# Gated MLP in a decode step's forward and backward pass: order of w2's rows, sums by row groups, and two vectors spread by matmuls of repeated columns

## The chip, the cores and the metric

The kernel runs on one core of one Trainium2 chip. The metric is the device time of one execution in microseconds (us); smaller is better. A core has TensorE (PE in the profile, its weight loads PEld), VectorE (DVE), ScalarE (ACT), GpSimd (POOL) and SyncE (SP, which here only issues transfers), and 16 DMA engines that move data between the chip's memory and the on-chip buffers. Matmul results land in PSUM, everything else lies in SBUF.

## The reference: what is computed

One token `x` (640 numbers) is normalised and goes through attention over a cache and through a gated MLP; both results are added to `x`. Then the gradients of this sum are taken with respect to nearly all inputs. Cut to what matters:

```python
xn  = layernorm(x)                                   # 1 x 640
q   = (xn @ wq) per head                             # 32 heads of 128
p   = softmax(q @ k_cache^T * 128**-0.5)             # 32 x 8192
o   = p @ v_cache
A   = o @ wo
gate, up = xn @ w1, xn @ w3                          # 1728 each
h   = silu(gate) * up
B   = h @ w2
out = x + A + B
# outputs: out, and the gradients of out (weighted by grad_out) for
# x, k_cache, v_cache, wq, wo, w1, w3, w2
```

`k_cache` and `v_cache` hold 32 x 8192 x 128 bf16 numbers each (67 MB), and so do their gradients. For the MLP, with `g = grad_out`: `dh = w2 @ g`, `dup = dh * silu(gate)`, `dgate = dh * up * silu'(gate)`, `dw2 = h x g`, `dw1 = xn x dgate`, `dw3 = xn x dup` (outer products), and `dxn = w1 @ dgate + w3 @ dup`.

## The kernel before

The instructions of each engine run in the order in which the program writes them (a manual schedule), so the text of the kernel is the order of every queue. There are three stages.

**Loads and set-up (L107 to L286).** SP issues loads in this order: x, w2 in two parts (L192, L193), w1 (L194), the last 64 rows of w2 (w2r, L195), w3 (L196), wq and wo of the first heads, K and V of heads 0 and 1, wq and wo of the next heads. F = 1728 = 13 x 128 + 64: the MLP's long axis is cut into NF = 13 blocks of 128 and a REST of 64, so NB = 14 columns hold a vector of 1728. Entry q of block b is element 13 q + b (`block`, L562). The rest is the last 64 elements. xn is kept as 5 columns of 128 (`xn_col`), NC = 5.

**MLP (L558 to L712).** The weights lie as [128, 5, 1728] (w1t, w3t) and [128, 13, 640] (w2t, with w2r beside it). In the order of the text:

- `dh_product` (L567): w2 times g on DVE, summed over columns by matmuls with the identity, three calls; the last one uses w2r. `dh_reduce` (L579) folds the sums into `dhc` (dh, 14 columns).
- `gate_sums` (L582): 70 matmuls with one moving column each, block by block, the five row groups `ci` inside; its weights are read from w1t with a step of 13 elements. Then tanh on ACT and small operations on DVE give silu and `dup`.
- `spread(1, dup, ...)` (L595): turns 14 columns into a row of 1728 that all partitions hold (`bc_sb`). DVE multiplies the identity by the repeated columns (L598, L600), which gives a wide diagonal `diag`; four matmuls with a weight of ones (L604) put its column sums on all partitions, in PSUM; ACT and DVE copy them to `bc_sb` (L605).
- `gate_sums` again, for `up` with w3; `dx_part(1, w3t, ...)` (L607): w3 times `bc_sb` on DVE (L609), summed by matmuls into `dx_ps` (L612); `keep_sums`, `dgate`; `spread(0, dgate, ())`, all copies on ACT; the rest of `dx_part(1, ...)`; `grad(1, w3t)` (L616, L618), which overwrites w3t with its gradient; the store of dw3 from POOL (L658) and the load of K for head 2 into the same buffers behind it (L659).
- `ps_out` (L664) for h @ w2, the w2 gradients on ACT (L622), `prep_steps(0)` (L289), which makes q and the gradient of o for heads 0 to 3, `dx_part(0, w1t, ...)`, `grad(0, w1t)`, and the store of dw1 (L693).

**Heads (L707 to L840).** For each of 32 heads, DVE multiplies K by q and V by the gradient of o in halves (`product`, L414), PE sums these by matmuls with the identity (L416), and softmax and its gradient follow. `outer` (L436 on DVE, L430 on ACT) writes the 2 MB gradients of V and K of this head to `ot` tiles; POOL stores them (L443). SP loads K three heads and V two heads ahead, as buffers come free. Four `ot` buffers exist, three for K and two for V. Some of them first hold what the MLP needs: w1t, w2t and w3t take K's buffers, and `dbc` (with diag, bc_sb and w2r) takes one of the `ot` buffers. The pool `ps_w` has three PSUM banks, which the MLP's sums take in turn; `ps_acc` has two, which the heads' products use.

At the end the last gradients and the two outputs of 640 are stored (L802 to L841).

Of the kernel before, what the change touches and what calls it, by code (L numbers as in the profile page):

```python
# [9 lines left out]
BF16 = mybir.dt.bfloat16  # L10
F32 = mybir.dt.float32
ALU = mybir.AluOpType
# [4 lines left out]
P = 128  # L17
# [4 lines left out]
def kernel(  # L22
# [22 lines left out]
    nc = tc.nc  # L45
# [3 lines left out]
    D = A_x.shape[2]  # L49
    F = B_w1.shape[1]  # L50
    assert DH == P and D % P == 0 and SK % (2 * P) == 0
    NC = D // P
# [8 lines left out]
    NF, REST = divmod(F, P)  # L61
    NB = NF + 1
# [4 lines left out]
    WIDE = 4  # L67
# [11 lines left out]
    opool = ctx.enter_context(tc.tile_pool(name="op", bufs=4))  # L79
    small = ctx.enter_context(tc.tile_pool(name="small", bufs=2))  # L80
    ps_pers = ctx.enter_context(tc.tile_pool(name="ps_pers", bufs=1, space=PSUM))
    ps_acc = ctx.enter_context(tc.tile_pool(name="ps_acc", bufs=2, space=PSUM))
    ps_s = ctx.enter_context(tc.tile_pool(name="ps_s", bufs=1, space=PSUM))
    ps_o = ctx.enter_context(tc.tile_pool(name="ps_o", bufs=1, space=PSUM))
    ps_w = ctx.enter_context(tc.tile_pool(name="ps_w", bufs=3, space=PSUM))
# [17 lines left out]
    with tc.manual_schedule(engines=ORDERED):  # L103
# [80 lines left out]
        w3t = kpool.tile([P, NC, F], BF16, name="w3t", tag="K")  # L184
        w1t = kpool.tile([P, NC, F], BF16, name="w1t", tag="K")
        w2t = kpool.tile([P, NF, D], BF16, name="w2t", tag="K")
        dbc = opool.tile([P, 4 * F + D], BF16, name="dbc", tag="o")
        diag = dbc[:, 0:2 * F].rearrange("p (w f) -> p w f", w=2)
        bc_sb = dbc[:, 2 * F:4 * F].rearrange("p (w f) -> p w f", w=2)
        w2r = dbc[:, 4 * F:]  # L190
        nc.gpsimd.memset(w2r, 0.0)
        nc.sync.dma_start(w2t[:, 0:W2A, :], w2_v[:, 0:W2A, :])  # L192
        nc.sync.dma_start(w2t[:, W2A:NF, :], w2_v[:, W2A:NF, :])  # L193
        nc.sync.dma_start(w1t[:], w1_v)  # L194
        nc.sync.dma_start(w2r[0:REST, :], B_w2[NF * P:F, :])  # L195
        nc.sync.dma_start(w3t[:], w3_v)  # L196
        load_wq(0)
        load_wo(0, nc.sync)
# [8 lines left out]
        ident_bf = consts.tile([P, P], BF16, name="ident_bf")  # L207
# [6 lines left out]
        ones_bf = consts.tile([P, P], BF16, name="ones_bf")  # L214
# [38 lines left out]
        xn_col_bf = consts.tile([P, NC], BF16, name="xn_col_bf")  # L253
# [4 lines left out]
        for i, row in enumerate((x_row, g_row)):  # L258
            for ci in range(NC):
                nc.tensor.matmul(ps_xg[:, 2 * i, ci:ci + 1], lhsT=row[:].rearrange("o (p c) -> o c p", c=NC)[:, ci, :],  # L260
                                 rhs=ones_bf[0:1, 0:1], start=True, stop=True)
                nc.tensor.matmul(ps_xg[:, 2 * i + 1, ci:ci + 1], lhsT=row[:, ci * P:(ci + 1) * P],
                                 rhs=ones_bf[0:1, 0:1], start=True, stop=True)
# [127 lines left out]
        def new_head(h):  # L391
            st = Head()
            st.h = h
            st.g, st.hh = divmod(h, GH)
            st.G = grp[st.g]
            st.K, st.V = kv_tiles.pop(h)
            hs[h] = st
            return st
# [163 lines left out]
        def block(ap, b):  # L562
            if b < NF:
                return ap[:, 0:NF * P].rearrange("p (q b) -> p b q", b=NF)[:, b, :]
            return ap[:, NF * P:F]
# [13 lines left out]
        def dh_reduce(b0, nb, dh_ps):  # L579
            nc.vector.tensor_reduce(dhc[:, b0:b0 + nb], dh_ps[:], AX.X, ALU.add)  # L580

        def gate_sums(name, wt):  # L582
            ps = ps_w.tile([P, NB], F32, name=name, tag="w")
            for b in range(NB):
                rows = P if b < NF else REST
                for ci in range(NC):
                    nc.tensor.matmul(ps[0:rows, b:b + 1], lhsT=block(wt[:, ci, :], b),
                                     rhs=xn_col_bf[:, ci:ci + 1], start=(ci == 0), stop=(ci == NC - 1))
            return ps

        def keep_sums(dst, ps):
            nc.vector.tensor_copy(dst[:, 0:NF], ps[:, 0:NF])
            nc.vector.tensor_copy(dst[0:REST, NF:NB], ps[0:REST, NF:NB])

        def spread(wi, vec, on_v):  # L595
            nc.vector.tensor_copy(dgu2[:, wi], vec)
            by_run = diag[:, wi, 0:NF * P].rearrange("p (q b) -> p q b", b=NF)
            nc.vector.tensor_tensor(by_run, ident_bf[:].unsqueeze(2).to_broadcast([P, P, NF]),  # L598
                                    dgu2[:, wi, 0:NF].unsqueeze(1).to_broadcast([P, P, NF]), ALU.mult)
            nc.vector.tensor_scalar(diag[:, wi, NF * P:F], ident_bf[:, 0:REST], vec[:, NF:NB], None, ALU.mult)  # L600
            for k in range(4):
                c = slice(k * F // 4, (k + 1) * F // 4)
                bc_ps = ps_w.tile([P, F // 4], F32, name="bc_ps", tag="w")
                nc.tensor.matmul(bc_ps[:], lhsT=ones_bf[:], rhs=diag[:, wi, c], start=True, stop=True)  # L604
                (nc.vector.tensor_copy if k in on_v else nc.scalar.copy)(bc_sb[:, wi, c], bc_ps[:])  # L605

        def dx_part(wi, wt, c0, n):  # L607
            T = tpool.tile([P, n, F], BF16, name="T13", tag="T")
# [16 lines left out]
        gate, up, th, sig, silu, hcol, t1, dgate, dup = (sm_f[:, i, :] for i in range(9))  # L625
        dhc = small.tile([P, NB], F32, name="dhc", tag="Pf")
        dgu2 = small.tile([P, 2, NB], BF16, name="dgu2", tag="Pf")
# [5 lines left out]
        dh2 = dh_product(2 * W2A, NB - 2 * W2A)  # L633
        dh_reduce(*dh1)
        dh_reduce(*dh2)
        keep_sums(gate, gate_sums("gate_ps", w1t))
        nc.scalar.activation(th, gate, ACTF.Tanh, scale=0.5)
        nc.vector.tensor_scalar(sig, th, 0.5, 0.5, ALU.mult, ALU.add)
        nc.vector.tensor_tensor(silu, gate, sig, ALU.mult)
        nc.vector.tensor_tensor(dup, dhc[:], silu, ALU.mult)  # L640
        spread(1, dup, (1, 3))
        nc.vector.tensor_scalar(t1, sig, -1.0, 1.0, ALU.mult, ALU.add)
        nc.vector.tensor_tensor(t1, t1, gate, ALU.mult)
        nc.vector.tensor_scalar(t1, t1, 1.0, None, ALU.add)
        nc.vector.tensor_tensor(t1, t1, sig, ALU.mult)
        nc.vector.tensor_tensor(t1, dhc[:], t1, ALU.mult)
        up_ps = gate_sums("up_ps", w3t)
        dx_ps = ps_w.tile([P, NC, DR1], F32, name="dx_ps", tag="w")
        dx_part(1, w3t, 0, 2)
        keep_sums(up, up_ps)  # L650
        nc.vector.tensor_tensor(dgate, t1, up, ALU.mult)
        nc.vector.tensor_tensor(hcol, silu, up, ALU.mult)
        nc.vector.tensor_copy(hcol_bf[:], hcol)
        spread(0, dgate, ())
        dx_part(1, w3t, 2, 2)
        dx_part(1, w3t, 4, 1)
# [4 lines left out]
        for b in range(NB):  # L661
            rows, src = (P, w2t[:, b, :]) if b < NF else (REST, w2r)
            for ci in range(NC):
                nc.tensor.matmul(ps_out[:, ci:ci + 1], lhsT=src[0:rows, ci * P:(ci + 1) * P],  # L664
                                 rhs=hcol_bf[0:rows, b:b + 1], start=(b == 0 and ci == 0), stop=(b == NB - 1),
                                 skip_group_check=True)
# [58 lines left out]
        for h in range(H - 1):  # L725
            n = new_head(h + 1) if h + 1 < H else None
            c = hs.pop(h)
# [51 lines left out]
        c = hs.pop(H - 1)  # L779
# [34 lines left out]
        for ci in range(NC):  # L814
            k, c = divmod(ci * P, WIDE_COLS)
# [56 lines left out]
```

## Time and profile before

| what | value |
|---|---|
| time, median of 3 runs | 720.65 us (719.62 to 720.72) |
| the profiled execution's own time | 720.15 us |
| its span, first to last instruction | 718.4 us |
| busy in the span: PE, DVE, ACT, POOL | 555.2, 631.4, 479.3, 49.5 us |
| moved by DMA | 303.32 MB, mean 422 GB/s |
| share of 16 DMA engines: SP's queue, POOL's queue, ACT's queue | 51.0%, 45.1%, 3.5% |
| mean granted clock of TensorE | 0.886 |
| dw3's store issued; dw1's store issued | 38.96 us; 46.54 us |
| first product of head 0 starts on DVE | 46.16 us |
| DVE's last instruction starts; last store issued | 707.99 us; 708.29 us |

How to read it: the busy share of an engine is an average over stages. The page's second part cuts the span into 40 slices of 18 us and gives for each the busy tenths of the engines and DMA and the rate. The fourth part follows the chain that ended last back from the end. The windows give the same numbers for stretches of one's own choice. A wait is given as who waited, for whom, how long in total, how often, and the longest.

### The profile page before, as it was taken

How to read it: one execution, taken by the hardware profiler on the slowest of the kernel's cores; microseconds unless marked ns; L12 is line 12 of the kernel's file. 1: busy time of each engine (PE TensorE's matmuls, PEld its weight loads, DVE VectorE, ACT ScalarE, POOL GpSimd, SP SyncE). 2: the span in 40 equal slices, each digit the busy share in tenths (PEclk: the TensorE clock that was granted, in tenths of full speed). 3: DMA queues.
4: the chain of work that ended last, by engine and by line, in shares of the span. 5: the costliest groups of instructions: out<-in, count | busy, mean ns of one | idle time of the engine just before them, and what ended most of it. 6: DMA issues, size and time to landing. Idle time of an engine off the chain costs nothing.

```text
span 718.4 us, 9840 instructions
## 1 busy us (share of the span) xinstructions
PE 555.2 (77%) x3516; PEld 274.3 (38%) x3516; DVE 631.4 (88%) x723; ACT 479.3 (67%) x1456; POOL 49.5 (7%) x91
## 2 busy tenths in 40 slices
PE   5787788888788786775888788497877888888862
PEld 3653343333344333332443344143433334333331
DVE  5789999999999996896799999499999989899992
ACT  2165677696779756695487866469677857678551
POOL 0010000000001210000000110000000000000100
PEclk9699989999998988997799979779899889999995
DMA  8999999999999999999999999999999999999997
GB/s 351 415 426 424 431 430 401 430 429 428 434 428 430 430 425 424 425 427 428 430 426 432 430 427 422 428 428 429 429 429 431 430 428 433 427 430 431 428 422 304
DMA packets 27694, 303.32 MB, mean 422 GB/s; under 512 B 3264, under 2 KB 3974, under 8 KB 9982
## 3 DMA queue, kind: packets, MB, share of 16 engines
q1 hardware_dynamic: 13490, 154.89, 51.0%
q0 software_dynamic: 10960, 137.72, 45.1%
q10 hardware_dynamic: 3196, 10.10, 3.5%
q8 instruction: 27, 0.44, 0.2%
q14 instruction: 21, 0.17, 0.1%
HBM read 151.34 MB, written 151.34 MB: 421 GB/s over the span
## 4 chain that ended last, share of the span: by engine, by line
DVE 41%; DMA 36%; PE 15%; ACT 5%; issue 1%; SPq 0%; POOL 0%; DVEq 0%; ACTq 0%; POOLq 0%
DMA Kt<-in_A_k_cache_dram 20%; DVE T L414 19%; DVE ot L436 12%; DMA out_dram<-ot 10%; DMA lane_pad<-in_A_wq_dram 4%; PE ob L485 4%; PE psDP L416 4%; ACT ot L430 3%; PE psS L416 3%; DMA dbc<-in_B_w_dram 2%; DVE S_sb L457 1%; DVE DP_sb L511 1%; PE ps_od L501 1%; PE dx_ps L612 1%; DVE P L476 1%
## 5 line engine op out<-in xcount | busy, mean ns | idle before, releaser
L416 PE MATMUL psDP<-T,ident_bf 128*128 128x512 bf16 x512 | 158.1, 465 | 67.4 <-DVE T L414 67.2
L416 PEld LDWEIGHTS <-ident_bf 128*128 128x128 bf16 x1024 | 107.9, 109 | 205.3 <-issue 131.1
L430 ACT ACTIVATE ot<-qs_g,Uf 128x128 bf16<-128x128 bf16 x496 | 151.7, 394 | 43.5 <-DVE Uf L523 26.5
L414 DVE TENSOR_TENSOR T<-Kt,qs_g 128x4096 bf16<-128x4096 bf16 x64 | 146.4, 2287 | 14.9 <-DMA Kt<-in_A_k_cache_dram 13.7
L430 ACT ACTIVATE ot<-do_g,Pf 128x128 bf16<-128x128 bf16 x504 | 154.0, 389 | 7.0 <-DMA out_dram<-ot 6.0
L414 DVE TENSOR_TENSOR T<-Vt,do_g 128x4096 bf16<-128x4096 bf16 x64 | 146.0, 2282 | 5.6 <-DMA Vt<-in_A_v_cache_dram 5.6
L416 PE MATMUL psS<-T,ident_bf 128*128 128x512 bf16 x512 | 126.4, 391 | 10.0 <-DVE T L414 10.0
L436 DVE TENSOR_TENSOR ot<-qs_g,U 128x3072 bf16<-128x3072 bf16 (+1 forms) x64 | 113.2, 1768 | 12.4 <-DMA out_dram<-ot 12.3
L436 DVE TENSOR_TENSOR ot<-do_g,P 128x3072 bf16<-128x3072 bf16 (+1 forms) x64 | 112.9, 1764 | 7.1 <-DMA out_dram<-ot 6.1
L443 POOL DMA_DIRECT2D out_dram<-ot x60 | 32.2, 536 | 548.4 <-DVE Uf L523 315.1
L485 PE MATMUL ob<-Vt,P 128*4 128x512 bf16 x512 | 62.2, 386 | 0.0
L485 PE MATMUL ob<-Kt,U 128*4 128x512 bf16 x512 | 60.5, 379 | 1.3 <-DVE U L518 1.3
L478 ACT ACTIVATE Pf<-E,rZ 128x16 f32<-128x16 f32 x32 | 9.7, 304 | 57.9 <-DVE rZ L474 57.9
L542 ACT ACTIVATE dq_diag<-ident_bf,odq 128x128 bf16<-128x128 bf16 x32 | 12.8, 401 | 50.9 <-DVE odq L538 50.9
L501 PEld LDWEIGHTS ps_od<-pick,wide 128*128 128x128 f32 x256 | 42.2, 233 | 8.3 <-issue 2.8
L501 PE MATMUL ps_od<-pick,wide 128*128 128x2 f32 x256 | 37.2, 267 | 0.5 <-ACT wide L493 0.5
L461 PE MATMUL sm<-ident_f,mrow 128*128 128x128 f32 x64 | 15.9, 331 | 24.1 <-DVE mrow L459 24.1
L485 PEld LDWEIGHTS <-U 128*4 128x4 bf16 x512 | 19.8, 84 | 37.4 <-DVE U L518 6.9
L485 PEld LDWEIGHTS <-P 128*4 128x4 bf16 x512 | 20.6, 85 | 24.7 <-issue 1.5
L493 ACT COPY wide<-ob 128x256 f32<-128x256 f32 x64 | 20.0, 362 | 10.5 <-PE ob L485 10.5
L306 ACT COPY woT<-ps_t 128x512 bf16<-128x512 bf16 x40 | 23.0, 576 | 5.2 <-PE ps_t L301 4.5
L457 DVE TENSOR_REDUCE S_sb<-psS 128x64 f32<-128x512 f32 x32 | 21.9, 685 | 4.5 <-PE psS L416 4.5
(173 smaller groups left out, 549.9 us busy)
## 6 DMA issues: line engine op xcount, KB each, us to landing
out_dram<-ot POOLq DMA_DIRECT2D x60, 2048.0 KB, 24.1
Kt<-in_A_k_cache_dram SPq DMA_DIRECT2D x32, 2048.0 KB, 26.5
Vt<-in_A_v_cache_dram SPq DMA_DIRECT2D x32, 2048.0 KB, 20.5
out_dram<-ot SPq DMA_DIRECT2D x8, 1024.0 KB, 13.3
out_dram<-wo_g ACTq DMA_DIRECT2D x6, 640.0 KB, 15.2
wo_g<-in_A_wo_dram ACTq DMA_DIRECT2D x6, 640.0 KB, 15.6
wq<-in_A_wq_dram SPq DMA_DIRECT2D x2, 1280.0 KB, 33.7
w1t<-in_B_w_dram SPq DMA_DIRECT2D x1, 2160.0 KB, 12.7
```

The costliest lines, as they stand in the source:

```text
L306: nc.scalar.copy(woT[:], ps_t[:])
L414: nc.vector.tensor_tensor(T[:], src[:, :, ds_], vec[:, ds_].unsqueeze(1).to_broadcast([P, J, DHH]), ALU.mult)
L416: nc.tensor.matmul(ps[:], lhsT=ident_bf[:], rhs=T[:, :, RUN * i:RUN * (i + 1)], start=(half == 0 and i == 0), stop=(half == 1 and i == DHH ...
L430: nc.scalar.activation(st.ot[half][:, JH - ACT_J + j].rearrange("p a b -> p (a b)"), vec, ACTF.Copy, scale=wf[:, half, j:j + 1])
L436: nc.vector.tensor_tensor(st.ot[half][:, 0:n], vec.rearrange("p (a b) -> p a b", b=2).unsqueeze(1).to_broadcast([P, n, DH // 2, 2]), w2[:, ...
L443: nc.gpsimd.dma_start(dst.rearrange("p j d -> p (j d)"), st.rows[:])
L457: nc.vector.tensor_reduce(st.S[:], st.ps["S"][:], AX.X, ALU.add)
L461: nc.tensor.matmul(st.sm[:, 8:8 + P], lhsT=mrow[:].to_broadcast([P, P]), rhs=ident_f[:], start=True, stop=True, skip_group_check=True)
L485: nc.tensor.matmul(ob[c0:c0 + WIDE, :], lhsT=w2[:, WIDE * q:WIDE * (q + 1), 0], rhs=src[:, WIDE * q:WIDE * (q + 1), :].rearrange("p j d -> ...
L493: nc.scalar.copy(part[:], ob[:, i * (WIDE // 2) * DH:(i + 1) * (WIDE // 2) * DH])
L501: nc.tensor.matmul(st.od, lhsT=st.wide[i][:, b * DH:(b + 1) * DH], rhs=pick[:, r, :], start=(r == 0), stop=(r == WIDE - 1), skip_group_che ...
L542: nc.scalar.activation(dq_diag[:], ident_bf[:], ACTF.Copy, scale=odq[:, 1:2])
```

## The change

Four edits, all in the loads and the MLP:

1. The load of w2's last rows (w2r) is issued before w1's, no longer after it.
2. `gate_sums` now runs the row groups `ci` outside and the 14 blocks inside, into a PSUM tile that the caller gives. For `up`, the first row group (14 matmuls) is issued right after the gate's sums, ahead of `spread(1, ...)`, and the other four (56) after it. `up_ps` now lies in the pool `ps_acc`.
3. `spread` builds no diagonal. For each of 13 blocks (and the rest) one matmul takes the column of that block, repeated 128 times, as weights, and the identity as the moving operand; four blocks share a PSUM bank. The sums are then copied to `bc_sb` with a step of 13 elements in the destination. The fourth chunk has one block and the rest, and two copies.
4. `dbc` loses the room for the diagonal.

```diff
-        dbc = opool.tile([P, 4 * F + D], BF16, name="dbc", tag="o")
-        diag = dbc[:, 0:2 * F].rearrange("p (w f) -> p w f", w=2)
-        bc_sb = dbc[:, 2 * F:4 * F].rearrange("p (w f) -> p w f", w=2)
-        w2r = dbc[:, 4 * F:]
+        dbc = opool.tile([P, 2 * F + D], BF16, name="dbc", tag="o")
+        bc_sb = dbc[:, 0:2 * F].rearrange("p (w f) -> p w f", w=2)
+        w2r = dbc[:, 2 * F:]
...
         nc.sync.dma_start(w2t[:, W2A:NF, :], w2_v[:, W2A:NF, :])
+        nc.sync.dma_start(w2r[0:REST, :], B_w2[NF * P:F, :])
         nc.sync.dma_start(w1t[:], w1_v)
-        nc.sync.dma_start(w2r[0:REST, :], B_w2[NF * P:F, :])
         nc.sync.dma_start(w3t[:], w3_v)
...
-        def gate_sums(name, wt):
-            ps = ps_w.tile([P, NB], F32, name=name, tag="w")
-            for b in range(NB):
-                rows = P if b < NF else REST
-                for ci in range(NC):
-                    nc.tensor.matmul(ps[0:rows, b:b + 1], lhsT=block(wt[:, ci, :], b),
-                                     rhs=xn_col_bf[:, ci:ci + 1], start=(ci == 0), stop=(ci == NC - 1))
-            return ps
+        def gate_sums(ps, wt, rows_of):
+            for ci in rows_of:
+                for b in range(NB):
+                    rows = P if b < NF else REST
+                    nc.tensor.matmul(ps[0:rows, b:b + 1], lhsT=block(wt[:, ci, :], b), rhs=xn_col_bf[:, ci:ci + 1],
+                                     start=(ci == 0 and b == 0), stop=(ci == NC - 1), skip_group_check=True)
...
         def spread(wi, vec, on_v):
             nc.vector.tensor_copy(dgu2[:, wi], vec)
-            by_run = diag[:, wi, 0:NF * P].rearrange("p (q b) -> p q b", b=NF)
-            nc.vector.tensor_tensor(by_run, ident_bf[:].unsqueeze(2).to_broadcast([P, P, NF]),
-                                    dgu2[:, wi, 0:NF].unsqueeze(1).to_broadcast([P, P, NF]), ALU.mult)
-            nc.vector.tensor_scalar(diag[:, wi, NF * P:F], ident_bf[:, 0:REST], vec[:, NF:NB], None, ALU.mult)
-            for k in range(4):
-                c = slice(k * F // 4, (k + 1) * F // 4)
-                bc_ps = ps_w.tile([P, F // 4], F32, name="bc_ps", tag="w")
-                nc.tensor.matmul(bc_ps[:], lhsT=ones_bf[:], rhs=diag[:, wi, c], start=True, stop=True)
-                (nc.vector.tensor_copy if k in on_v else nc.scalar.copy)(bc_sb[:, wi, c], bc_ps[:])
+            by_block = bc_sb[:, wi, 0:NF * P].rearrange("p (q b) -> p b q", b=NF)
+            for k, b0 in enumerate(range(0, NF, WIDE)):
+                n = min(WIDE, NF - b0)
+                bc_ps = ps_w.tile([P, WIDE, P], F32, name="bc_ps", tag="w")
+                for b in range(b0, b0 + n):
+                    nc.tensor.matmul(bc_ps[:, b - b0, :], lhsT=dgu2[:, wi, b:b + 1].to_broadcast([P, P]), rhs=ident_bf[:],
+                                     start=True, stop=True, skip_group_check=True)
+                if b0 + n == NF:
+                    nc.tensor.matmul(bc_ps[:, n, 0:REST], lhsT=dgu2[:, wi, NF:NB].to_broadcast([P, P]),
+                                     rhs=ident_bf[:, 0:REST], start=True, stop=True, skip_group_check=True)
+                copy = nc.vector.tensor_copy if k in on_v else nc.scalar.copy
+                copy(by_block[:, b0:b0 + n, :], bc_ps[:, 0:n, :])
+                if b0 + n == NF:
+                    copy(bc_sb[:, wi, NF * P:F], bc_ps[:, n, 0:REST])
...
-        keep_sums(gate, gate_sums("gate_ps", w1t))
+        gate_ps = ps_w.tile([P, NB], F32, name="gate_ps", tag="w")
+        gate_sums(gate_ps, w1t, range(NC))
+        keep_sums(gate, gate_ps)
+        up_ps = ps_acc.tile([P, NB], F32, name="up_ps", tag="acc")
+        gate_sums(up_ps, w3t, range(1))
         nc.scalar.activation(th, gate, ACTF.Tanh, scale=0.5)
...
-        up_ps = gate_sums("up_ps", w3t)
+        gate_sums(up_ps, w3t, range(1, NC))
         dx_ps = ps_w.tile([P, NC, DR1], F32, name="dx_ps", tag="w")
```

## The prediction

> **What bounds the kernel now.** I read the page first, then the windows, then DVE's waits. The page's slices, bytes and chain:
>
> ```profile
> DVE  5789999999999996896799999499999989899992
> DMA  8999999999999999999999999999999999999997
> GB/s 351 415 426 424 431 430 401 430 429 428 434 428 430 430 425 424 425 427 428 430 426 432 430 427 422 428 428 429 429 429 431 430 428 433 427 430 431 428 422 304
> HBM read 151.34 MB, written 151.34 MB: 421 GB/s over the span
> DVE 41%; DMA 36%; PE 15%; ACT 5%; issue 1%; SPq 0%; POOL 0%; DVEq 0%; ACTq 0%; POOLq 0%
> ```
>
> The DMA row is 9 in every slice but the first and the last, and the rate stands near 428 GB/s from the second slice to the last but one. The DVE row has holes, at 6, 4 and 8. The last line is only one chain, and its DVE share says that DVE often ended last, not that DMA was free then. The windows (columns: PE, PEld, DVE, ACT, POOL busy us, granted clock, DMA share, GB/s) show both at once:
>
> ```profile
> 60.00:245.00 185.00, 152.55 (x932) 72.05 (x932) 180.35 (x195) 138.48 (x436) 13.64 (x24) 0.93 1.01 427
> 400.00:500.00 100.00, 76.38 (x449) 36.71 (x448) 85.53 (x94) 69.54 (x215) 9.55 (x15) 0.86 1.01 427
> 110.00:115.00 5.00, 4.86 (x35) 2.63 (x34) 5.00 (x5) 5.00 (x17) 0.00 (x0) 1.00 0.98 374
> 705.00:710.00 5.00, 1.65 (x7) 1.25 (x7) 1.57 (x11) 0.00 (x0) 0.00 (x0) 0.50 1.00 413
> 710.00:719.00 9.00, 0.00 (x0) 0.00 (x0) 0.00 (x0) 0.00 (x0) 0.00 (x0) 0.50 0.42 161
> ```
>
> DVE is 97% busy from 60 to 245 us and 86% busy from 400 to 500, yet DMA moves 427 GB/s in both. So DMA does not wait for compute: transfers lie queued (the page's issues: a 2 MB tile lands 20 to 27 us after its issue, though 2.1 MB at 427 GB/s take 4.9). From 250 us on compute waits for DMA:
>
> ```profile
> DVE ot L436 <- DMA out_dram<-ot: 18.4, 4, 9.9
> DVE T L414 <- DMA Kt<-in_A_k_cache_dram: 13.2, 9, 3.7
> DVE T L414 <- DMA Vt<-in_A_v_cache_dram: 5.6, 1, 5.6
> ```
>
> That is 37.2 us of DVE standing idle for transfers, against 0.5 us for a K tile between 60 and 245. The end belongs to DMA too: no engine computes after 708.3 us, and the store of out_1, issued at 708.10, lands 8.5 us later (SP's wait at the end) behind stores queued before it. A lone small transfer (x_row, issued at 0.74, used at 2.24) takes 1.5, so the last computation could be some 7 us later and the end stay. Thus the time is 303.32 MB at DMA's rate, plus 2 us before the first packet, plus the thin last slice. The change leaves all bytes as they are.
>
> **The change, step by step: how far ahead compute comes.** All of it lies in the first 60 us. DVE in that stretch:
>
> ```profile
> 15.22 0.49 DVE L572 TENSOR_TENSOR T<-dbc,g_bc_bf 128x640 bf16<-128x640 bf16 x1 [1.97 <-DMA dbc<-in_B_w_dram]
> 22.08 1.89 DVE L598 TENSOR_TENSOR dbc<-ident_bf,dgu 128x1664 bf16<-128x1664 bf16 x1
> 27.16 1.95 DVE L609 TENSOR_TENSOR T<-w3t,dbc 128x3456 bf16<-128x3456 bf16 x1
> 30.87 1.89 DVE L598 TENSOR_TENSOR dbc<-ident_bf,dgu 128x1664 bf16<-128x1664 bf16 x1
> ```
>
> *w2r ahead of w1.* The 1.97 us wait for w2r goes: the 80 KB now come behind w2, in use at 9.14, so by about 9.5, and L572's product runs at 13.2. What is late next is w1: landed 12.7 us after its issue at 2.02, so 14.7; the issue of w2r on SP (0.79 us) now stands ahead of it, and of w3's not (it was there already). DMA has w2's 2.1 MB (5 us) to do meanwhile, so I charge w1 only the 80 KB, 0.2 us. The 70 gate matmuls (16.51 to 20.72, 4.2 us) start at 15.0 instead of 16.51 and end at 19.2: 1.5 us gained.
>
> *Row groups.* The same 140 matmuls at 62 ns. Fourteen of the up sums now stand on PE ahead of the spread, 0.87 us, and add a wait for w3: SP's wait for w3's landing ended at 20.15. Queued behind them are the spread's matmuls, for which ACT and DVE wait. So PE is free at 21.0, and the gate's small DVE chain (1.34 us from 20.71 to 22.05 before) is ready at 20.55; the wait costs 0.45 us. If w3 landed later, this step would slip one for one.
>
> *Spread of dup.* Off DVE go 1.89 + 0.23 us (L598, L600). PE does 14 matmuls of 128 columns: the transposes at L301 have that shape, 4 in 0.39 us at full clock and 0.59 at half; the clock here is 0.50, so 0.6 a chunk. The copies out of PSUM write with a step of 13 elements, which no row shows. Bounds: 0.58 us for 512 columns on ACT without a step (L315) and 1.30 with a step of 4 (L332); a step of 13 when read as weights costs 157 to 166 ns against 96 (L587, L664), 1.7 times, so 1.30 x 1.7 = 2.2 at worst. I take 1.30, the nearest in kind; on DVE between 0.72 (L605's 0.61 for 432, scaled) and 2.2. ACT has chunks 0 and 2: 21.6 + 2.6 = 24.2. DVE has chunk 1, then the fourth chunk, whose matmuls wait for chunk 0's buffer (23.0), then five small operations (1.0 us): 24.8. The product L609 starts at 24.8 instead of 27.16.
>
> [...]
>
> *Up sums and dgate.* The other 56 matmuls (3.5 us) follow the fourth chunk at 23.3 and end at 26.8, about when L609 ends (26.7). The 0.92 us wait at 30.03 nearly goes; the chain to the bf16 copy (0.82 us) ends at 27.65, and DVE goes straight to L609 on w3, without a second L598 and L600: 27.7 instead of 32.83, 5.1 us ahead. dw3's store leaves at 33.9 instead of 38.96.
>
> *Spread of dgate.* It lies beside 2.92 us (L609) and 2.98 (L618) of DVE, until 33.5. PE comes to it after 18 dx matmuls, at 29.7; ACT does all copies, 3 x 1.30 and some 0.7, from 30.3 to 34.9 (before: 1.89 us in all). So DVE waits 1.4 us, and the lead falls to 38.56 - 34.9 = 3.6 us. With 0.58 a copy nothing waits and it is 5.1; with 2.2 it is about 0.5. The same copies hold PE's ps_out and ACT's w2 gradients, which come only about 1.3 us earlier; qs_g (42.0 before) is still ready before DVE's first product at 46.16 - 3.6 = 42.6.
>
> *The smaller dbc tile and up_ps in the other PSUM pool* cost nothing: dbc's pool gives buffers of the 2 MB tiles' size, and the bank is free until psS, after up_ps has been read.
>
> **The sum.** Compute enters the heads 3.6 us (0.5 to 5.1) ahead. From 60 to 245 us it keeps that; then K tiles and stored buffers do not come sooner, because DMA was full all along, and DVE's 37.2 us of waits become about 41. On the end: 0. From the profiled execution, 720.15 us (span 718.4 and 1.75 around it): 720.15. The median of the runs is 0.5 above; I put 720.4, between the two.
>
> **Rivals.**
>
> *The lead reaches the end.* For it: DVE 41% of the chain, and DVE 97% busy to 245 us. Then 720.4 - 3.6 = 716.8, or half of that if only the stretches at 406 GB/s (45 to 50, 55 to 60) fill up and the last slice packs tighter. Against it: 37.2 us of waits for DMA stand between, ten times the lead. 19%.
>
> *Slower: another slow patch in DMA.* Between 105 and 115 us DMA ran at 397 and 374 GB/s with its engines busy (shares 1.04 and 0.98), while loads and stores ran together; at 427 it would have moved 0.42 MB more: 1.0 us, which a DMA-bound kernel pays in full. Stores that leave 3.6 to 5 us sooner meet other loads. One more patch: 721.4; two: 722.4, and slower counts from the second on. Against it: one patch in 700 us. 13%.
>
> *The copies cost 2.2 us or more, so the change does not do what it says.* The lead is then 0.5 or below zero; the end is the same by the same cover. It would need some 15 us of delay to empty DMA's queue (20 us of landing less 4.9). This is 15 of the 68% below.
>
> **The numbers.** No difference at the end: 68%, by itself 719.2 to 721.7 (the three runs span 1.1 us, and I add the 0.5 between profile and median). Faster 19%, slower 13%. The range takes in one and a half patches above (722.1) and two thirds of the lead below (718.0). Faster and slower count beyond 0.2%, 1.4 us, about what a measurement of this kernel can tell from no change.
>
> **What would show it.** Right: the diagonal product gone; K's first product at 42 to 43 us instead of 46.16; dw3's store near 34; DVE's waits for DMA after 245 us up by about the lead; DMA at 9 in the same slices. Wrong in the steps: stepped copies far from 1.30 us on ACT; PE waiting for w3 beyond 20.2. Wrong in the end: a span shorter by the lead with DVE's waits unchanged, or a new stretch below 400 GB/s.

## The result, and the profile after

Before takes 719.71 us (median of 10 executions, 719.20 to 720.95), the changed kernel 721.85 us (10 executions, 721.19 to 726.33): a ratio of 1.0030, 95% interval 1.0018 to 1.0042. It is **slower by 2.1 us**, where no difference was forecast. The profiled execution of the changed kernel took 721.23 us, with a span of 719.4 us and a mean granted clock of 0.898. It is one of the shorter ones; its difference to the profiled execution of before is 1.1 us, half of that between the medians. A longer one was traced at the end (below).

The page of the changed kernel, its slices of DMA:

```profile
DMA  8999999999999999999999999999999999999997
GB/s 355 418 415 426 432 414 401 431 430 425 430 433 427 429 426 421 433 428 427 430 432 427 432 421 424 429 428 427 430 433 429 431 428 428 432 430 430 428 422 295
```

The DMA row has the digits of before. The rate does not: the third slice has 415 (before 426), the sixth 414 (431), the seventh 401 in both. In windows of 20 us (columns as in the prediction; the last two are DMA share and GB/s), the changed kernel, and then before:

```profile
60.00:80.00 20.00, 14.99 (x93) 7.16 (x92) 19.75 (x19) 11.76 (x40) 1.52 (x3) 1.00 1.00 422
...
100.00:120.00 20.00, 16.75 (x109) 8.09 (x108) 19.72 (x21) 15.03 (x46) 1.06 (x2) 0.98 1.00 397
...
400.00:700.00 300.00, 228.57 (x1397) 107.48 (x1397) 269.67 (x294) 211.01 (x657) 21.98 (x37) 0.92 1.01 428
```

```profile
60.00:80.00 20.00, 14.65 (x91) 6.88 (x91) 19.72 (x21) 12.03 (x40) 1.06 (x2) 1.00 1.02 433
...
100.00:120.00 20.00, 17.57 (x109) 8.22 (x107) 19.58 (x24) 15.42 (x48) 1.06 (x2) 0.93 1.00 405
```

The share is 1.00 at 397 GB/s and 1.01 at 428. The share counts the time that packets take; where a packet takes longer, the engines look as busy and move less. So here this row did not tell a full queue from slow packets, and the digit 9 that carried the forecast says less than it seemed to.

Counting the bytes that have landed by a given time, the changed kernel is level with before until 95 us (within 0.3 us, at 427 GB/s), is 0.65 us behind at 105, 0.75 behind at 125, and 0.64 behind at 700. What is lost is lost in heads 0 to 3, and nothing gives it back or adds to it.

Where compute went. DVE of the changed kernel, 26 to 52 us, then ACT:

```profile
26.55 1.96 DVE L611 TENSOR_TENSOR T<-w3t,dbc 128x3456 bf16<-128x3456 bf16 x1 [0.32 <-ACT dbc L605]
...
29.26 1.95 DVE L611 TENSOR_TENSOR T<-w3t,dbc 128x3456 bf16<-128x3456 bf16 x1
...
40.09 3.83 DVE L611 TENSOR_TENSOR T<-w1t,dbc 128x3456 bf16<-128x3456 bf16 x2 [4.48 <-ACT dbc L607]
45.60 1.06 DVE L611 TENSOR_TENSOR T<-w1t,dbc 128x1728 bf16<-128x1728 bf16 x1 [1.68 <-PE dx_ps L614]
...
49.48 2.28 DVE L413 TENSOR_TENSOR T<-Kt,qs_g 128x4096 bf16<-128x4096 bf16 x1
```

```profile
21.82 4.70 ACT L605 CAST dbc<-bc_ps 128x512 bf16<-128x512 f32 x2 [1.54 <-PE bc_ps L599]
32.09 7.44 ACT L605 CAST dbc<-bc_ps 128x512 bf16<-128x512 f32 x4 [5.57 <-PE bc_ps L599]
```

The diagonal is gone, and the second product on w3 starts 3.6 us sooner (29.26, before 32.83). Then DVE waits 4.48 us for ACT: two stepped copies of 512 columns take 4.70 us, **2.35 each**, and the four of the second spread 7.44. Head 0's first product starts at 49.48 instead of 46.16: compute enters the heads 3.3 us late, not 3.6 early. From 245 us on DVE waits for DMA as much as forecast:

```profile
DVE T L413 <- DMA Kt<-in_A_k_cache_dram: 19.1, 12, 4.2
DVE ot L435 <- DMA out_dram<-ot: 17.6, 4, 8.0
DVE T L413 <- DMA Vt<-in_A_v_cache_dram: 4.1, 1, 4.1
```

These are 40.8 us (37.2 before). That sum was forecast for a lead; it came with a lateness, so it shows neither.

### The profile page after: what moved, and what is told of

Its sections match the earlier page's. It is cut to its first block, busy times and chain, and to the rows that moved or that the text cites. A ratio compares the mean times of both kernels' runs of the same rounds, so it can differ in the third digit from the quotient of the medians.

```text
span 719.4 us, 9878 instructions
## 1 busy us (share of the span) xinstructions
PE 550.4 (77%) x3536; PEld 272.3 (38%) x3536; DVE 629.5 (88%) x720; ACT 488.6 (68%) x1457; POOL 49.5 (7%) x91
## 2 busy tenths in 40 slices
DMA packets 27694, 303.32 MB, mean 422 GB/s; under 512 B 3264, under 2 KB 3974, under 8 KB 9982
## 4 chain that ended last, share of the span: by engine, by line
DMA 38%; DVE 34%; PE 21%; ACT 5%; issue 1%; POOL 0%; DVEq 0%; ACTq 0%; POOLq 0%
DMA Kt<-in_A_k_cache_dram 25%; DVE T L413 17%; DVE ot L435 11%; DMA out_dram<-ot 10%; PE psS L415 5%; PE ob L484 4%; PE psDP L415 4%; DMA lane_pad<-in_A_wq_dram 4%; ACT ot L429 2%; PE dx_ps L614 1%; DVE S_sb L456 1%; DVE DP_sb L510 1%; PE ps_od L500 1%; ACT dbc L605 1%; PE dh_ps L574 1%
## 5 line engine op out<-in xcount | busy, mean ns | idle before, releaser
L415 PE MATMUL psDP<-T,ident_bf 128*128 128x512 bf16 x512 | 150.5, 447 | 69.2 <-DVE T L413 69.2
L415 PE MATMUL psS<-T,ident_bf 128*128 128x512 bf16 x512 | 129.8, 399 | 20.7 <-DVE T L413 20.7
L500 PEld LDWEIGHTS ps_od<-pick,wide 128*128 128x128 f32 x256 | 36.7, 206 | 7.5 <-issue 2.2
L500 PE MATMUL ps_od<-pick,wide 128*128 128x2 f32 x256 | 32.5, 249 | 0.5 <-ACT wide L492 0.5
```

Of the source, the lines that this page charges most:

```text
L415: nc.tensor.matmul(ps[:], lhsT=ident_bf[:], rhs=T[:, :, RUN * i:RUN * (i + 1)], start=(half == 0 and i == 0), stop=(half == 1 and i == DHH ...
L500: nc.tensor.matmul(st.od, lhsT=st.wide[i][:, b * DH:(b + 1) * DH], rhs=pick[:, r, :], start=(r == 0), stop=(r == WIDE - 1), skip_group_che ...
```

## The experiments

Theories at the start. **A:** the lateness of compute is the loss, because DMA's queue in heads 0 to 3 is thin and not 15 us deep. **B:** something that the change moved (the early stores, the load order, the stepped writes) disturbs DMA by itself, and the lateness is harmless. The table gives for each run the start of head 0's first product on DVE; the bytes at 125 us against before's trace (in us at 427 GB/s, plus is ahead); the profiled execution's time; the median and the ratio to before with its interval. In all traces but one (marked) the gap in bytes moves by at most 0.5 us between 125 and 700 us.

| run | first product | bytes at 125 us | profiled | median | ratio |
|---|---|---|---|---|---|
| before | 46.16 | 0 | 720.15 | 719.71 | |
| changed | 49.48 | -0.75 | 721.23 | 721.85 | 1.0030 [1.0018, 1.0042] |
| e1_old_spread | 44.68 | -0.3 | 721.64 | 720.07 | 1.0006 [0.9994, 1.0018] |
| e2_new_spread | 50.11 | -1.25 | 721.12 | 722.91 | 1.0057 [1.0037, 1.0077] |
| d1_late3 | 48.50 | -1.75 | 721.67 | 721.86 | 1.0031 [1.0019, 1.0043] |
| f1_blocks_inside | 42.87 | -1.0 | 721.00 | 720.93 | 1.0021 [1.0006, 1.0036] |
| x1_v3_later | 45.40 | +1.3, gone by 400 us | 720.81 | 720.10 | 1.0004 [0.9993, 1.0015] |
| s1_late3_halves | 49.98 | -6.9 | 728.62 | 728.54 | 1.0110 [1.0090, 1.0129] |
| v2_elsewhere_late | 48.10 | -1.0 | 721.61 | 722.50 | 1.0032 [1.0019, 1.0045] |
| d3_late9 | 54.53 | -8.0 | 728.37 | 728.23 | 1.0108 [1.0088, 1.0129] |
| x2_after_v3_later | 49.92 | -1.3 | 721.50 | 722.75 | 1.0044 [1.0027, 1.0060] |
| x3_blocks_v3_later | 42.63 | -3.5 | 724.40 | 721.51 | 1.0023 [1.0012, 1.0034] |
| a1_after_again | 49.67 | -1.1 | 721.53 | - | |
| a2_after_again | 53.63 | -7.35 | 727.55 | - | |

Three things are to be seen in it. The profiled time less 720.15 follows the bytes at 125 us within 0.6 us in nine of the rows (a2: 7.4 against 7.35; d3: 8.2 against 8.0) and within 2.0 in the others (x1, whose gain goes back, is the worst). A late first product loses in every run, and an early one gains in none; f1, early by 3.3 us, is slower than before with an interval that leaves out no change. And the start of head 0 does not give the size of the loss (2.3 us late lose 1.75 us of bytes in d1, 4.0 lose 1.25 in e2), but a later moment does: when SP issues the load of V of head 4, at 106.48 us in before. The traces have this issue late by 0.8 us (changed), 0.3 (e1), 1.4 (e2), 1.7 (d1), 1.2 (f1), 1.3 (v2), 8.2 (d3), 1.2 (x2), 3.9 (x3), 1.0 (a1) and 7.4 (a2), which is the loss in bytes within 0.4 us in each. x1 does not fit (2.2 early), and in s1 this load is cut in two.

### The two halves of the change

e1_old_spread is the changed kernel with the spread of before (and the room for its diagonal in `dbc`); the early w2r and the row groups stay (excerpt):

```diff
-            by_block = bc_sb[:, wi, 0:NF * P].rearrange("p (q b) -> p b q", b=NF)
+            by_run = diag[:, wi, 0:NF * P].rearrange("p (q b) -> p q b", b=NF)
...
+                nc.tensor.matmul(bc_ps[:], lhsT=ones_bf[:], rhs=diag[:, wi, c], start=True, stop=True)
```

e2_new_spread is the kernel before with the new spread and the smaller `dbc`, and nothing else (the same lines the other way round).

> The changed kernel with the old spread (diagonal, one matmul of ones per chunk, contiguous copies); w2r's early load and the row groups stay. Theory 'late': the changed kernel is slower because its stepped copies (2.37 us on ScalarE for 512 columns) bring compute into the heads 3.3 us later, and the early stage cannot take that without loss. Then this one, with head 0's first product near 44.4 us (46.16 before, 49.48 changed), is not slower than before: 719 to 720 us. Rival 'order': the new order of loads or sums costs by itself; then about 721.8. Rival 'chance of the patch' (a stretch near 100 to 116 us where some loads' packets take 750 ns instead of 611, in both profiles; what it costs depends on which loads meet it): either way by up to 1 us, with V3's or K5's load slow in the profile.

> The kernel before with the new spread alone (repeated columns, stepped copies); old order of loads and sums. Theory 'late': head 0's first product near 50.5 us, 1 us later than in the changed kernel, so at least as slow: 722 to 723 us. Rival 'order': as before, 719.7. Rival 'stepped writes disturb transfers while they run' (20 to 40 us): DMA rate between 20 and 40 us below 420 GB/s, and the time up even though the heads are level.

e1 starts head 0 1.5 us ahead of before and takes the same time; e2 starts it 4.0 us behind and loses 3.2 us (719.71 to 722.91). So the spread alone (with its smaller `dbc`) carries the loss, and the other two edits make no difference that these runs can tell. This does not yet tell lateness from the writes themselves.

### Lateness without the change

d1_late3 is before, with the gradient of w1 computed twice. Nothing else is touched:

```diff
         grad(0, w1t)
+        grad(0, w1t)
```

> The kernel before, with dw1's gradient (5 instructions on VectorE, 2.98 us) computed a second time, so that only the heads and dw1's store start 3 us later; nothing of the change is in it. Theory 'late': as the changed kernel, 721.5 to 722.5 us, and the bytes moved fall behind those of before by some 0.6 us between 60 and 115 us. Rival 'cover' (my prediction): 719.7, no difference. Rival 'order' or 'stepped writes': 719.7 as well.

Head 0 starts 2.3 us late, and the kernel takes 721.86 us, ratio 1.0031: the loss of the changed kernel (721.85, 1.0030) without any part of the change. B falls as it stands: lateness is not harmless, and the loss needs no early store of dw3 and no stepped write. The store of dw1, with the load of K of head 3 behind it, is late together with the heads in both kernels (48.88 and 49.85 us, before 46.54); no run takes these two apart. d3_late9 gives a larger dose (four times, head 0 8.4 us late).

> The kernel before with dw1's gradient computed four times: the heads start 8.9 us later. Theory 'late, by a thin queue around 90 to 115 us': V3 and V4 are issued later still, the load queue is dry for longer, and the loss grows beyond 2.2 us, to 724 or more. Rival 'one fixed patch': 721.9 as with 3 us. By my prediction's cover of some 15 us: 719.7.

It takes 728.23 us. Its windows:

```profile
60.00:80.00 20.00, 15.05 (x85) 6.21 (x82) 17.04 (x18) 7.56 (x26) 0.53 (x1) 0.97 0.88 353
80.00:100.00 20.00, 15.39 (x96) 7.55 (x98) 19.68 (x23) 13.95 (x47) 1.07 (x2) 1.00 1.00 406
100.00:120.00 20.00, 18.06 (x105) 9.09 (x105) 19.47 (x21) 13.54 (x44) 1.07 (x2) 0.83 0.96 347
```

Here even the share drops, to 0.88: part of the time DMA has nothing to do. Of 8.4 us of lateness 8.0 are lost in bytes. The cover that the prediction put at some 15 us is what is not lost: 0.6 us in d1 (2.3 late, 1.75 lost), 0.4 in d3, 2.7 in e2 and 2.6 in the changed kernel (3.3 late, 0.75 lost in that trace).

### The copies made cheap

f1_blocks_inside is the changed kernel with the copies' loops exchanged: four blocks, which lie side by side in the destination, run inside, the 128 entries outside. The same numbers go to the same places.

```diff
-            by_block = bc_sb[:, wi, 0:NF * P].rearrange("p (q b) -> p b q", b=NF)
+            by_block = bc_sb[:, wi, 0:NF * P].rearrange("p (q b) -> p q b", b=NF)
...
-                copy(by_block[:, b0:b0 + n, :], bc_ps[:, 0:n, :])
+                copy(by_block[:, :, b0:b0 + n], bc_ps[:, 0:n, :].rearrange("p b q -> p q b"))
```

> The changed kernel with the copies out of PSUM running over the four blocks of a chunk inside and the 128 entries outside, so that four bf16 lie side by side in SBUF before the next step of 13; same bytes, same matmuls. If the step of single elements in the write is what costs, a copy of 512 columns takes about 1.2 us instead of 2.37 and head 0's first product starts near 45.5 us; theory 'late' then gives 719 to 720.5 us. If the copies stay at 2.4 us, the time stays at 721.9.

ACT of f1:

```profile
21.98 1.69 ACT L605 CAST dbc<-bc_ps 128x512 bf16<-128x512 f32 x2 [1.54 <-PE bc_ps L599]
...
30.50 2.67 ACT L605 CAST dbc<-bc_ps 128x512 bf16<-128x512 f32 x4 [6.83 <-PE bc_ps L599]
```

A copy takes 0.85 us instead of 2.35, and head 0 starts at 42.87, 3.3 us ahead: the lead that the prediction worked out (3.6) exists once the copies cost what it took them for, or less. It buys nothing: 720.93 us is 1.2 us above before (ratio 1.0021, interval 1.0006 to 1.0036). So taking the lateness at head 0 away does not take the whole loss away. DVE of f1 between 40 and 140 us has a wait that before has not:

```profile
DVE T L413 <- DMA Vt<-in_A_v_cache_dram: 4.7, 1, 4.7
```

It ends at 91 us, and at 4.7 us it is longer than the lead. The V tile is issued sooner than in before (63.08 us, before 67.69) and does not land sooner: the first store of a head's gradient leaves sooner too (65.22 us, before 69.83), and by 85 us stores have moved 1.0 MB more than in before and loads 1.0 MB less. So the lead has become a lateness when V of head 4 is issued (107.6 us, before 106.5), and f1 loses 1.0 us of bytes like a late kernel.

### Where DMA loses it

The trace's DMA packets, counted by tile (loads of 128 packets of 16 KB), mean ns of one:

| tile | before | changed | e2 | d1 | e1 | f1 | x1 | v2 | x2 |
|---|---|---|---|---|---|---|---|---|---|
| V of head 3 | 611 | 659 | 711 | 727 | 616 | 611 | 612 | 662 | 621 |
| V of head 4 | 746 | 750 | 750 | 773 | 760 | 798 | 611 | 778 | 728 |

Nearly all other loads have means of 611 to 633. At 109 and 110 us of before, 23 and 16 packets of V of head 4 start per microsecond, at 749 and 906 ns, and no store beside them; otherwise loads and stores together are about 26 a microsecond, at 611. My second theory was that a load that starts on an empty load queue is slow. x1_v3_later tried it on before: V of head 3 is issued behind a 20-byte copy that waits for head 2's exponentials, so that the load queue runs empty at 98 us (for 1.2 us), while stores go on.

```diff
-            if h + 2 < H:
+            if h + 2 < H and h != 1:
...
                 exps(n)
+                if h == 1:
+                    nc.sync.dma_start(xm[0:1, :], n.E[0:1, 0:NC])
+                    load_v(h + 2)
```

> The kernel before, compute untouched; only the load of V for head 3 is issued later, about 95.5 us instead of 90.6, behind a 20-byte copy on SyncE that waits for head 2's exponentials (the copy goes to a tile that nothing reads any more). Theory 'dry load queue': the loss comes from V3's load being issued after K4's has run out (94.5 us), so that it runs with nothing beside it and its packets take 700 ns and more instead of 611; then V3's mean packet is over 650 ns here and the time goes up by 0.5 to 2 us although VectorE enters the heads on time. Rival 'lateness of compute itself' (stores late too): the time stays at 719.7, unless head 3 waits for V3.

Neither tile is slow (612, 611), so an empty load queue alone is not the cause. Nor is it enough that a transfer runs alone: stores without a load beside them run at 611 to 613 (before at 106 us, the changed kernel at 94 to 95), and so does a load without a store (x2 at 107, 108 and 111 us). And V of head 3 in the changed kernel is slow at 101 to 103 us (753, 669 and 737 ns) with 11 or 12 store packets a microsecond beside it. DMA is 1.3 us ahead from 115 us on, and gives it back between 340 and 400 us, where it runs at 424 GB/s (before 429) and DVE is 91% busy. The time is that of before.

v2_elsewhere_late is d1, with heads 3 and 4 reading V of heads 11 and 12 (the results of those two heads are then of other values), to see whether the addresses matter:

```diff
-            nc.sync.dma_start(Vt[:], vc[h])
+            nc.sync.dma_start(Vt[:], vc[h + 8 if h in (3, 4) else h])
```

> The late kernel, but heads 3 and 4 read V of heads 11 and 12 (so the results of heads 3 and 4 are those of other values). If the slow packets belong to the addresses of V3 and V4, they are gone and the time falls to 719.7 or below; if they belong to the moment and the empty queue, V3's and V4's packets stay near 730 and 770 ns and the time at 721.9.

The same loads are slow at 662 and 778 ns from other addresses, and the time stays (722.50 us): not the addresses.

s1_late3_halves is d1 with these two loads cut into two of 64 partitions each, so that two are in flight:

```diff
-                nc.sync.dma_start(Vt[:], vc[h])
+                n_part = 2 if h in (3, 4) else 1
+                for i in range(n_part):
+                    rows = slice(i * P // n_part, (i + 1) * P // n_part)
+                    nc.sync.dma_start(Vt[rows], vc[h][rows])
```

> The late kernel (dw1's gradient computed twice, 3 us late, 721.86) with the loads of V for heads 3 and 4 each issued as two transfers of 64 partitions. If a single transfer in flight is what runs slow, two in flight go at 611 ns a packet and the time comes back toward 720. If loads that start on an idle load queue run slow whatever their number, or their addresses do, it stays at 721.9.

A miss: 728.54 us, with V of head 3 at 1013 ns a packet and V of head 4 at 851. The test was confounded. Head 0 started 1.5 us later than in d1, and 1.8 us of bytes were lost by 80 us, before the first half load; the other 5 came from 100 us on. Whether the halved loads or the thin queue made the 1013 ns (727 in d1), no run here takes apart.

x2_after_v3_later and x3_blocks_v3_later put x1's move into the changed kernel and into f1.

> The changed kernel with one move: the load of V of head 3 is issued behind a 20-byte copy of head 2's exponentials, so at about 98 to 100 us instead of 93.5, where the stores of head 1's gradients are in flight beside it. Theory A (the loss of the change is made where a V tile crosses alone): V3's packets, 659 ns in the changed kernel, come back to 611, DMA's bytes at 125 us stand at least 0.5 us above those of the changed kernel, and part of the loss of 2.1 us goes: 720.4 to 721.4. Theory B (V3's patch is only where the lateness shows; the lateness itself is what costs, since the loads and stores of heads 0 to 3 are released by late compute): the bytes come out the same by 125 us whatever V3's packets take, and the time stays at 721.4 to 722.2.

> The changed kernel with the copies' blocks inside (compute 3.3 us ahead of before at head 0) and the load of V of head 3 behind the same 20-byte copy. In the run without that move the lead was lost in a wait of 4.7 us for a V tile at 91 us, with the time at 720.9. If a lead can reach the end at all once no V tile crosses alone, the time is 717.5 to 719.3. If DMA bounds the run from head 4 on whatever compute does before, it is 719.3 to 721.0, the same as before.

In x2 V of head 3 crosses at 621 ns, as the first theory in its expectation wanted, and nothing is won: bytes -1.3 at 125 us, 722.75 us. Now the last packets of head 1's dK store run alone, at 911 ns around 103 us. The slow packets have moved from a load to a store. The test is weaker than it was meant to be: the last packet of the load before ends at 94.8 us and the first of V of head 3 at 104.5, so that the move also left the load queue empty for nearly 10 us (share 0.94 at 374 GB/s in that stretch, x1 1.00 at 426). That V of head 3 is only where the lateness shows, and not part of what it costs, is therefore not shown. x3 has the lead of f1 and, in the trace of its longest execution, loses it in a longer wait:

```profile
DVE T L413 <- DMA Vt<-in_A_v_cache_dram: 6.9, 1, 6.9
```

Its time is 721.51. No version here beats before.

### Two more traces of the changed kernel

> The changed kernel once more, unchanged, for a second trace of it: its first trace is of an execution of 721.23 us and shows DMA 0.7 us behind before, while the median over ten runs is 2.1 us behind. If the whole loss is made where heads 0 to 3 leave DMA thin, a trace of an execution of 722 us or more is 1.5 to 3 us behind in bytes by 125 us and level from there to 700 us. If part of it comes elsewhere, the bytes fall behind after 125 us, or the execution is longer with the bytes no further behind than 0.7 us.

> The same as the run before, a third trace of the changed kernel. The same two readings: bytes 1.5 to 3 us behind by 125 us and level from there where the execution is 722 us or longer, or a loss after 125 us.

a1 (721.53 us) repeats the first trace with bytes -1.1. a2 is an execution of 727.55 us, like the 726.33 of the timed runs: head 0 starts at 53.63 us, bytes are 7.35 behind at 125 us and 7.48 at 700. PE of a2:

```profile
21.37 1.09 PE L585 MATMUL up_ps<-xn_col_bf,w3t 128*128 128x1 bf16 x14 [1.59 <-DMA w3t<-in_B_w_dram]
...
35.78 0.38 PE L599 MATMUL bc_ps<-ident_bf,dgu 128*128 128x128 bf16 x4 [2.24 <-ACT dbc L605]
38.02 0.27 PE L599 MATMUL bc_ps<-ident_bf,dgu 128*128 128x128 bf16 x1 [1.85 <-ACT dbc L605]
...
46.63 3.09 PE L614 MATMUL dx_ps<-T,ident_bf 128*128 128x192 bf16 x18
```

Windows of a2 (the first number after the POOL column is the granted clock), and of the first trace of the changed kernel:

```profile
34.00:36.00 2.00, 0.22 (x4) 0.21 (x4) 2.00 (x4) 2.00 (x2) 0.00 (x0) 1.00 1.00 418
...
40.00:44.00 4.00, 4.00 (x83) 3.94 (x82) 2.69 (x2) 0.81 (x3) 0.00 (x0) 0.50 1.00 427
44.00:48.00 4.00, 3.78 (x32) 2.52 (x31) 1.14 (x1) 3.24 (x6) 0.56 (x1) 0.50 0.98 414
```

```profile
40.00:44.00 4.00, 4.00 (x95) 3.37 (x93) 3.83 (x2) 0.94 (x2) 0.00 (x0) 0.93 0.99 421
44.00:48.00 4.00, 4.00 (x61) 4.00 (x60) 2.40 (x4) 4.00 (x8) 0.56 (x1) 1.00 1.04 438
```

Two things add up to 4 us. PE waits 1.59 us for w3 before the first row group, which moves everything behind it by 1.2. Then TensorE's clock: it stood at 1.00 at 34 to 36 us, PE waited twice for stepped copies (2.24 and 1.85 us, with 0.38 of work between), and the clock fell to 0.50 (0.66 on average at 36 to 38 us) and stayed there until about 50 us. The 18 dx matmuls take 3.09 us where they take 1.65 at full clock, and DVE waits 4.62 us for them instead of 1.68. In before the clock is at 1.00 from 34 to 56 us.

The fall in a2 lies within these two waits (4.1 us together); that the waits caused it was not shown. In before the clock also goes from 1.00 to 0.50, at 18.9 us, with PE busy since 15.8. The way back differs between the traces: in the first one of the changed kernel PE is busy from 36.8 us, with full clock at about 40.5 (0.86 on average at 40 to 42); in a2 PE was busy from 38.0 us with one gap of 0.22, and the clock took some 12 us.

So the dear copies cost some 3.3 us of lateness in each of the three traces, and in one of them 2.9 more came with PE's clock, which fell during the waits for them; the 1.2 by w3's landing are not theirs. Whether every execution above 726 us (one of ten timed ones of the changed kernel, three of ten of e2) has this cause was not shown; one was traced.

## Why the prediction was wrong, by its steps

**Bounds: "Thus the time is 303.32 MB at DMA's rate" and "DMA was full all along".** Wrong between 75 and 125 us, and this is the step that decided the end. The depth was read from landing times of the whole run, 20 to 27 us. In the stage where it mattered, loads of V in before between 60 and 140 us:

```profile
L122 SPq DMA_DIRECT2D Vt<-in_A_v_cache_dram x4: 327/328/328, 67.7 to 124.8; - x4
...
DMA to landing us min/median/max: 11.5/13.8/16.2
```

SP's waits in before, 60 to 112 us:

```profile
SPq L122 <- PE ob L485: 39.2, 3, 21.1
```

Even 13.8 us is not a backlog of 9. Loads share DMA with stores there (some 13 of 26 packets a microsecond), so that 2.1 MB take about 10 us without any queue. And 16 us pass between two issues of V (90.6 and 106.5 us): the next load is issued only after its buffer was released by compute, PE's last use of the V tile two heads back, for which SP waits. **"The copies cost 2.2 us or more … the end is the same by the same cover … some 15 us of delay"** is where it failed outright: 2.35 us a copy came, and the cover was 0.4 to 2.7 us (0.1 in a2: 7.5 late, 7.35 lost).

**"On the end: 0."** Right for a lead, which is what it was said of, in that none gains: e1 comes 1.5 us ahead and takes the time of before. It is not nothing for a larger one: f1 comes 3.3 us ahead and is 1.2 us slower. The reason was another, too: the lead ends in a wait for a V tile at 91 us, not in the waits after 245 us.

**"I take 1.30, the nearest in kind"** (bounds 0.58 and 2.2). The term that turned a lead into a lateness: 2.35 us on ACT, above the upper bound, and on DVE 3.09 us for a full copy and the 128 columns of the fourth chunk, with 0.42 for the rest. The factor of 1.7 came from weight reads on PE, another engine and direction. On ACT a step of 4 already cost 1.30 against 0.58 in before, and the step of 13 cost 1.8 times that. f1 shows the remedy: with four neighbours written in a row, 0.85 us.

**"So DVE waits 1.4 us".** It waited 4.48 us, and then 1.68 more that no step named. PE's queue holds the last dx matmuls, `ps_out` and `prep_steps` behind the spread's matmuls, and these wait 2.07 and 1.66 us for ACT's copies:

```profile
34.55 0.58 PE L599 MATMUL bc_ps<-ident_bf,dgu 128*128 128x128 bf16 x4 [2.07 <-ACT dbc L605]
36.80 0.27 PE L599 MATMUL bc_ps<-ident_bf,dgu 128*128 128x128 bf16 x1 [1.66 <-ACT dbc L605]
...
36.93 4.15 PE L614 MATMUL dx_ps<-T,ident_bf 128*128 128x192 bf16 x36
```

By the prediction's sum at 2.2 us a copy the lead would still have been 0.5 us. It came out at -3.3: ACT began the second spread at 32.09 us and not at 30.3, which with the copies brought DVE to w1's products at 40.09 us (before 38.56), 1.5 us late, and the wait of 1.68 us came on top.

**w2r ahead of w1.** The wait is gone (the product runs at 13.07; forecast 13.2), the gate's matmuls start at 14.78 (15.0). They end at 19.76, not 19.2, since the new order takes 4.98 us for the 70 instead of 4.36 (e1, with the new order, 5.09; e2, with the old one, 4.24): 0.9 us gained, not 1.5.

**Row groups.** PE is free at 20.94, forecast 21.0. "If w3 landed later, this step would slip one for one" came true in a2: a wait of 1.59 us, and the spread 1.2 later.

**Product times.** First product on w3 at 26.55 (forecast 24.8), second at 29.26 (27.7), dw3's store at 35.93 (near 34): late by two dear copies, still ahead of before.

**The rival "another slow patch".** It had the right place (V of heads 3 and 4) and another cause than the runs show: it put a patch down to stores that leave sooner, and the first store of a head's gradient leaves later in the changed kernel (71.82 us, before 69.83). Its price of 1.0 us a patch was about right for d1 and too high for the changed kernel: by an estimate from the packet times, 128 packets over 16 engines, V of head 3 costs 0.9 us more at 727 ns and 0.4 at 659. V of head 4 is slow in every kernel of the table but x1, before included; V of head 3 is slow in the four late ones (659 to 727 ns) and not where compute is on time or early (611 to 616), so the second patch comes with the lateness. Whether it is part of the price or only goes with it stays open, since x2, which took it away, left the load queue empty instead.

## What to carry to other kernels

A busy share of 1.0 did not show here how much was queued: read the landing time in the stage in question, subtract what sharing with other queues explains, and look whether the next issue waits for a buffer that compute releases. Where it does, look how late that issue comes, not how late the stage begins: here each microsecond of it cost nearly one, and a lead at the start had turned into a lateness by then, so that a change of the set-up could lose and no version won. In the medians, a start 2 to 4 us late cost 2.1 to 3.2 us (s1, with its cut loads, aside), and one 8.4 us late 8.5. A PSUM copy with a step in its destination has to be priced by its own run length and step (0.58, 0.85, 1.30 or 2.35 us for 512 columns on ACT here); exchanging the loops so that neighbours are written in a row is the cheap form.

## What the runs showed of the hardware that was not expected

- A copy of 128x512 from PSUM to bf16 on ACT: 2.35 us with a step of 13 elements, 0.85 with four neighbours and then a jump of 13, against 0.58 without a step and 1.30 with a step of 4 in the trace of before. At 0.85, four neighbours with a step of 13 beat single elements with a step of 4.
- Packets of 16 KB, 611 ns nearly everywhere, take 650 to 1230 ns on average over single microseconds in places between 99 and 114 us (the range of before and the changed kernel): in before with no store beside the load (906 ns at 110 us), in the changed kernel with some 12 store packets beside it (753 ns at 101 us), and at the end of a store (911 ns in x2). The address is not the cause (v2), an empty load queue by itself is not (x1, and x2 with 621 ns after nearly 10 us of it), and lone stores and lone loads can also run at 611. What makes them slow stays open.
- TensorE's granted clock stayed at 0.50 for some 12 us of nearly unbroken work after two waits of 2.24 and 1.85 us, in one of three traced executions. With a wait for a load, the same program differed by 4 us there.
